# Warm-up, first transposes and one block fewer in halves: four small edits at the start of a fused convolution and two-layer kernel

## The chip, the cores and the metric

The kernel runs on one core of a Trainium2 chip. The metric is the device time of one execution in microseconds. A profile gives the span from the first to the last instruction, which is about 2 us less than the time of the same execution.

## The reference

A causal convolution of seven taps over the sequence, one set of softmax-normalised taps for each of eight heads, and then two matrix products with a leaky ReLU between them.

```python
w = softmax(weight, axis=-1)                       # 8 heads, 7 taps
out[b, s, h, :] = sum_k w[h, k] * x_pad[b, s + k, h, :]   # x: 8 x 4096 x 192
h = out.reshape(32768, 192) @ w_in                 # 192 x 2048
y = maximum(0.01 * h, h) @ w_out                   # 2048 x 192, fp32 out
```

## The kernel before

The sequence is cut into 32 blocks; a block is 512 positions of two batch rows. The first blocks are worked in halves of 256 positions, so that the first matmuls can start before much of x has arrived. After these the kernel passes to whole blocks and to another form of the second product.

```python
NHALF = 4
groups = [(b, h * HT, HT) for b in range(NHALF) for h in range(2)]
groups += [(b, 0, ST) for b in range(NHALF, NBLK)]
# ...
plan = {0: [0] * 4, NSW - 2: [16, 8, 8, 16], NSW - 1: [8, 8, 16, 16],
        NSW: [16, 8, 8, 16, 8, 8, 16, 16]}         # NSW = 2 * NHALF
```

At the very start TensorE runs warm-up matmuls while x and the taps are loaded. Then it selects the taps (a matmul with a 0/1 matrix spreads them over 128 partitions), transposes the first x into PSUM, and convolves the first half block by matmuls with diagonal matrices. VectorE and ScalarE build these diagonals and copy the transposed x out of PSUM.

```python
warm(6, ST)                          # six matmuls of 512 columns
select(wps_hm, slice(0, 2)); warm(1, 128)
select(wps_l, 2);            warm(1) # 256 columns
# ... casts of x, whm <- wps_hm
diag_wide(0, 0, K); diag_each(1, 1, range(2))
transpose_first(0)                   # six transposes 128x128, bf16 in PSUM
warm(1, ST)
evac_first(0, nc.scalar.copy, nc.vector.tensor_copy)
diag_wide(0, 1, K)                   # VectorE
for p in range(2): diag_wide(2, p, K)
spread_down(0)                       # VectorE, w_in within SBUF
# ... wml, rsum (VectorE): every evacuation of the convolution needs rsum
diag_each(1, 1, range(2, K)); diag_each(1, 0, range(K))   # ScalarE
# ... convolution: 84 matmuls; evac_0(act_scale), evac_2(...), evac_1(act_scale)
```

A "unit" is a group of twelve first-layer matmuls, followed by one ScalarE activation of 128x1024 (Prelu, PSUM to g). Two PSUM buffers `ph` are shared by the units. The third piece of x is transposed behind unit 7, the last of the first half block.

Of the kernel before, what the change touches and what calls it, by code (L numbers as in the profile page):

```python
# [10 lines left out]
FP32 = mybir.dt.float32  # L11
BF16 = mybir.dt.bfloat16
# [3 lines left out]
def kernel(  # L16
# [8 lines left out]
    nc = tc.nc  # L25
# [11 lines left out]
    NCH = D // CH  # L37
# [3 lines left out]
    HS = SUB // 2  # L41
    NFC = F // 128
    NB = S // ST
    NBLK = (B // 2) * NB
    NHALF = 4
    RUN = 4
    NPEC = 3
    FIRST = (0, 2, 1)
# [12 lines left out]
    psum_o = ctx.enter_context(tc.tile_pool(name="po", bufs=4, space=bass.MemoryType.PSUM))  # L61
# [5 lines left out]

    groups = [(b, h * HT, HT) for b in range(NHALF) for h in range(2)]
    groups += [(b, 0, ST) for b in range(NHALF, NBLK)]

# [34 lines left out]
    def new_xt(rp):  # L105
        xt[rp] = xt_pool.tile([128, NCH, HALO + S], BF16, name="xt")
        nc.vector.memset(xt[rp][:, :, 0:HALO], 0.0)
# [5 lines left out]
    x_half = {  # L113
        q: const_pool.tile([128, NCH, HS, 2, CH], BF16, name=f"x_half{q}") for q in (0, 3)
    }
# [27 lines left out]
    ptr = {}  # L143

    def transpose_first(q):
        n = HS if q == 0 else 1
        ts = [
            psum_o.tile([128, HS // n, NCH, 128], BF16, name=f"ptr{i}", tag="po")
            for i in range(n)
        ]  # L150
        for s in range(HS):
            t = ts[s * n // HS]
            for c in range(NCH):
                if q == 0:
                    nc.tensor.transpose(
                        out=t[:, 0, c, :],
                        in_=x_half[q][:, c, s, :, :].rearrange("p e k -> p (e k)"),
                        identity=ident,
                    )
                    continue  # L160
                for e in range(2):
                    nc.tensor.transpose(  # L162
                        out=t[e * CH : (e + 1) * CH, s, c, :],
                        in_=x_rows[q][:, e, s, c * CH : (c + 1) * CH],
                        identity=ident,
                    )
        ptr[q] = [t[:, s] for t in ts for s in range(HS // n)]

    def evac_first(q, *copies):
        dst = xt[0][:, :, HALO + q * HT : HALO + (q + 1) * HT]  # L170
        dst = dst.rearrange("p c (s k) -> p s c k", s=HS)
        for s, t in enumerate(ptr.pop(q)):
            copies[s](out=dst[:, s], in_=t)  # L173
# [13 lines left out]
    def conv_jobs(grp, chunks=range(NCH)):  # L187
        blk, t0, T = grp
        rp, st = divmod(blk, NB)
        if blk not in yt:  # L190
            yt[blk] = yt_pool.tile([128, NCH, ST], BF16, name="yt")
        y = yt[blk]
        jobs = []
        for k in range(K):
            for c in chunks:
                a = BASE + k + st * ST + t0
                src = xt[rp][:, c, a : a + T]
                dst = y[:, c, t0 : t0 + T]
                if k == 0:
                    jobs.append(  # L200
                        lambda s=src, d=dst, c=c: nc.vector.tensor_scalar_mul(  # L201
                            d, s, wk[:, c, 0:1]
                        )
                    )
                else:
                    jobs.append(
                        lambda s=src, d=dst, c=c, k=k: nc.vector.scalar_tensor_tensor(  # L207
                            out=d, in0=s, scalar=wk[:, c, k : k + 1], in1=d,
                            op0=mybir.AluOpType.mult, op1=mybir.AluOpType.add,
                        )  # L210
                    )
        return jobs
# [42 lines left out]
    def run(*lists):  # L255
        for slots in zip_longest(*lists, fillvalue=()):
            for both in slots:
                for job in both:
                    job()
# [31 lines left out]
    def spread_down(n):  # L291
        nc.vector.tensor_copy(out=w_in[n][0:CH, 1, :], in_=w_in[n][CH:128, 0, :])

    def spread_up(n):
        nc.vector.tensor_copy(out=w_in[n][CH:128, 1:3, :], in_=w_in[n][0:CH, 0:3:2, :])
# [10 lines left out]
    ident = const_pool.tile([128, 128], BF16)  # L306
# [3 lines left out]
    for rows in (0, 128):  # L310
# [7 lines left out]
        in_=moe_w_out.rearrange("(c p i) d -> p c i d", p=128, i=RUN),  # L318
# [7 lines left out]
    def warm(n, cols=HT):  # L326
        for _ in range(n):
            nc.tensor.matmul(  # L328
                out=wa[:, 0, 0:cols], lhsT=ones[:, 0:128], rhs=ones[:, 0:cols],
                start=True, stop=True,  # L330
            )
# [21 lines left out]
    ident2 = const_pool.tile([128, CH], BF16)  # L353
    nc.vector.tensor_add(ident2, ident[:, 0:CH], ident[:, CH:128])
    warm(6, ST)
    wps = psum_h.tile([128, 2, ST], FP32, name="wps", tag="ph")
    wps_hm = wps[:, 0, 0 : NCH * 2 * (K + 1)].rearrange("p (c q k) -> p c q k", c=NCH, q=2)
    wps_l = wa[:, 1, 0 : NCH * (K + 1)].rearrange("p (c k) -> p c k", c=NCH)

    def select(out, parts):  # L360
        for c in range(NCH):
            for e in range(2):
                nc.tensor.matmul(
                    out=out[e * CH : (e + 1) * CH, c], lhsT=sel[:, c, :],
                    rhs=w9p[:, parts, :], start=True, stop=True,
                )
# [1 line left out]
    select(wps_hm, slice(0, 2))  # L368
    warm(1, 128)
    select(wps_l, 2)  # L370
    warm(1)
    new_xt(0)
    cast_first(0, 0, nc.scalar.copy)
    cast_first(0, 1, nc.scalar.copy, slice(0, 1))
# [22 lines left out]
    diag_wide(0, 0, K)  # L397
    diag_each(1, 1, range(2))
    transpose_first(0)
    warm(1, ST)  # L400
    evac_first(0, nc.scalar.copy, nc.vector.tensor_copy)
# [38 lines left out]
    g, po, acc2, osb, seal = {}, {}, {}, {}, None  # L440
    NSW = 2 * NHALF
    subs = [
# [148 lines left out]
    def evac_o(n):  # L591
# [4 lines left out]
        o_sb = osb[n if n >= LAST else n - n % 2]  # L596
        copy = nc.scalar.copy if b < NHALF else nc.vector.tensor_copy
        ins = copy(out=o_sb[:, n % 2, :], in_=po.pop(n))  # L598
# [18 lines left out]
    for i, grp in enumerate(groups):  # L617
        blk, t0, T = grp
        steps = T // 64
        if t0 == 0:  # L620
            g[blk] = g_pool.tile([128, NFC, 2, ST], BF16, name="g", tag="g")
        quota = plan.get(i, [16] * 4 if T == HT else [5, 5, 6, 5, 5, 6, 8, 8])

        if i == 0:
            ahead = []
        else:
            ahead = conv_jobs(groups[i + 1]) if i + 1 < len(groups) else []
        per = -(-len(ahead) // steps)
        for j in range(steps):
            for u in range(2 * j, 2 * j + 2):  # L630
                mm1(grp, u, 128 if i <= NSW else CH)
                if i == 0 and u == 0:
                    conv_1 = conv_jobs(groups[1], (1,))
                    for job in conv_1[:3]:
                        job()
                    spread_down(1)
                    spread_up(1)
                    for job in conv_1[3:]:
                        job()
                    pe_0, evac_0 = pe_conv_jobs(groups[1], 0)  # L640
                    pe_2, evac_2 = pe_conv_jobs(groups[1], 2, cross=True)
                if i == 0 and u in CUTS:
                    cut = slice(*CUTS[u])
                    run(pe_0[cut], pe_2[cut])
                if i == 0 and u == 5:
                    evac_0(nc.vector.tensor_scalar_mul)
                    evac_2(nc.vector.tensor_scalar_mul, nc.vector.tensor_scalar_mul)
                if i == 0 and u == 7:
                    transpose_first(2)
            jobs = ahead[per * j : per * (j + 1)]  # L650
            if T == ST:


                jobs = ahead[len(ahead) * j // steps : len(ahead) * (j + 1) // steps]
                for job in jobs:
                    job()
                jobs = []
            for _ in range(quota[j]):
                if i <= NSW:
                    mm2_row_slot(slot)  # L660
                else:
                    mm2_slot(slot)
                slot += 1
            if i == 0 and j == 3:
                evac_first(2, nc.vector.tensor_copy, nc.vector.tensor_copy)
            if i == 2 and j == 1:
                transpose_x(2)
            for job in jobs:
                job()
            if i == 0 and j == 3:  # L670
                transpose_half(3)

            last_half = t0 + T == ST
            if i == NSW and j == steps - 1:
                evac_o(LAST - 1)
                slot = NSW * NR * NFC
            if j == steps // 4 and last_half:
                load_x(blk + 3)
            if j == steps // 2 and last_half and blk > 0:
                transpose_x(blk + 2)  # L680
# [35 lines left out]
```

## Time and profile before

| quantity | value | from |
|---|---|---|
| time | 685.11 us (684.30, 685.11, 686.15) | three timed runs |
| span of the profiled execution | 682.4 us (its time: 684.35) | profile |
| TensorE busy | 677.2 us | profile |
| first second-layer matmul starts | 19.77 us | timeline |
| a half block, steady | 10.52 us | window |
| a whole block, steady | 20.72 us | window |

TensorE is the bound, busy 677.2 of 682.4 us: everything after the first 20 us is matmul after matmul. Two questions are left for a change like this one: does it shorten the sum of matmuls, and does it bring the first second-layer matmul forward? The lines that show this are in the prediction below.

### The profile page before, as it was taken

The page shows a single profiled execution, that of the slowest core. Times are in us where ns is not written, and L with a number is a line of the kernel's source. Part 1 is how long each engine was busy: PE and PEld are TensorE (multiplying, and loading weights), DVE is VectorE, ACT ScalarE, POOL GpSimd, SP SyncE. Part 2 cuts the span into 40 slices and gives each one's busy share as a digit, 9 for nine tenths or more (in the row PEclk, how much of TensorE's full clock was granted, in tenths as well). Part 3 has the DMA queues.
Part 4 walks back from the last instruction along what each step waited for, and adds up shares of the span by engine and source line. Part 5 has one row for each costly group of instructions (what it writes and reads, how often), then busy time and mean ns, then how long its engine had stood idle before and what let it go on. Part 6 is the DMA issues. An engine that isn't in the chain of part 4 may idle for free.

```text
span 682.4 us, 27404 instructions
## 1 busy us (share of the span) xinstructions
PE 677.2 (99%) x12575; PEld 467.1 (68%) x12575; DVE 481.4 (71%) x845; ACT 524.2 (77%) x623; POOL 145.9 (21%) x204
## 2 busy tenths in 40 slices
PE   9999999999999999999999999999999999999998
PEld 6999987666666666666666666666666666666667
DVE  7979767667678667687667786676786676876612
ACT  7888998778777777777778777777777777777781
POOL 7722223222102222012222022221022220000000
PEclk9999999999999999999999999999999999999999
DMA  9965668556467557376565575574575573321123
GB/s 152 109 91 74 84 90 88 68 56 91 78 89 86 63 65 93 73 96 78 57 79 82 85 95 68 56 91 79 88 87 62 66 95 71 72 56 34 33 49 93
DMA packets 211763, 53.29 MB, mean 78 GB/s; under 512 B 205120, under 2 KB 211264, under 8 KB 211648
## 3 DMA queue, kind: packets, MB, share of 16 engines
q0 software_dynamic: 98736, 13.97, 31.0%
q1 hardware_dynamic: 112896, 37.57, 27.5%
q8 instruction: 98, 1.61, 1.0%
q14 instruction: 17, 0.14, 0.1%
q10 hardware_dynamic: 16, 0.00, 0.0%
HBM read 28.31 MB, written 25.17 MB: 78 GB/s over the span
## 4 chain that ended last, share of the span: by engine, by line
PE 97%; ACT 2%; DVE 0%; issue 0%; ACTq 0%
PE ph L461 48%; PE acc L550 41%; PE po L487 7%; ACT g L468 1%; PE acc L232 1%; PE ptr L162 0%; ACT L334 0%; ACTq L263 0%; ACT diag L391 0%; ACT xt L173 0%; DVE o_sb L598 0%; DVE x_half L138 0%; ACT w L340 0%; ACT junk L334 0%; DVE w9p L348 0%
## 5 line engine op out<-in xcount | busy, mean ns | idle before, releaser
L468 ACT ACTIVATE g<-ph 128x1024 bf16<-128x1024 f32 x512 | 496.2, 1021 | 136.4 <-PE ph L461 136.0
L207 DVE SCALAR_TENSOR_TENSOR yt<-xt,wk,yt 128x512 bf16<-128x512 bf16 (+1 forms) x618 | 382.9, 691 | 0.2
L461 PE MATMUL ph<-yt,w_in 64*64 64x512 bf16 (+2 forms) x6048 | 378.0, 363 | 0.7 <-ACT g L468 0.5
L550 PE MATMUL acc<-g,w_out 64*64 64x512 bf16 x5184 | 316.5, 376 | 0.0
L461 PEld LDWEIGHTS <-w_in 64*64 64x64 bf16 (+1 forms) x6048 | 239.1, 129 | 96.9 <-issue 2.8
L550 PEld LDWEIGHTS <-w_out 64*64 64x64 bf16 x5184 | 168.4, 119 | 108.4
L83 POOL DMA_DIRECT2D x_bf<-in_x_dram x180 | 134.1, 770 | 412.0 <-DMA xt<-x_bf 303.8
L572 DVE STREAM_TRANSPOSE o_t<-acc 128x512 f32<-128x512 f32 x81 | 67.2, 866 | 171.1 <-PE acc L550 171.1
L487 PE MATMUL po<-w_out,g 64*128 64x192 bf16 (+1 forms) x1152 | 60.1, 243 | 0.0
L487 PEld LDWEIGHTS <-g 64*128 64x128 bf16 (+1 forms) x1152 | 55.7, 94 | 1.6 <-issue 0.4
L201 DVE TENSOR_SCALAR yt<-xt,wk 128x512 bf16<-128x512 bf16 (+1 forms) x103 | 28.1, 322 | 14.5 <-DMA xt<-x_bf 14.4
L560 ACT COPY junk<-junk 128x1 f32<-128x1 f32 x54 | 10.4, 192 | 4.1 <-ACT g L468 0.4
L598 ACT COPY o_sb<-po 128x192 f32<-128x192 f32 x32 | 10.1, 320 | 1.3
L598 DVE COPY o_sb<-po 128x192 f32<-128x192 f32 x8 | 2.8, 356 | 6.8 <-PE po L487 4.0
L232 PE MATMUL acc<-xt,diag 64*64 64x256 bf16 x140 | 5.5, 272 | 0.4 <-ACT xt L173 0.4
L232 PEld LDWEIGHTS <-diag 64*64 64x64 bf16 x140 | 4.3, 106 | 1.5 <-DVE xt L173 0.7
L132 POOL DMA_DIRECT2D x_half<-in_x_dram x6 | 4.2, 720 | 1.2 <-DMA w_in<-in_moe_w_in_dram 1.2
L328 PE MATMUL warm<-const-bfloat16-1.0 128*128 128x512 bf16 (+2 forms) x9 | 3.6, 515 | 0.8 <-PEq L700 0.8
L391 ACT ACTIVATE diag<-ident,whm 128x64 bf16<-128x64 bf16 x14 | 3.5, 337 | 0.2 <-DVE whm L377 0.2
L128 POOL DMA_DIRECT2D x_rows<-in_x_dram x4 | 3.0, 751 | 0.0
L173 DVE COPY xt<-ptr 128x384 bf16<-128x384 bf16 x5 | 1.6, 352 | 1.8 <-PE ptr L162 1.7
L334 ACT ACT_TABLE_LOAD x1 | 1.3, 1283 | 1.4 <-PEq L700 1.4
(45 smaller groups left out, 22.5 us busy)
## 6 DMA issues: line engine op xcount, KB each, us to landing
out_dram<-o_t SPq DMA_DIRECT2D x108, 192.0 KB, 4.7
x_bf<-in_x_dram POOLq DMA_DIRECT2D x180, 64.0 KB, 3.3
out_dram<-o_sb SPq DMA_DIRECT2D x16, 192.0 KB, 3.2
xt<-x_bf SPq DMA_TRANSPOSE x90, 3.8
w_out<-in_moe_w_out_dram POOLq DMA_DIRECT2D x1, 768.0 KB, 9.4
out_dram<-o_sb SPq DMA_DIRECT2D x8, 96.0 KB, 1.9
w_in<-in_moe_w_in_dram POOLq DMA_DIRECT2D x2, 256.0 KB, 5.5
x_nat<-in_x_dram SPq DMA_DIRECT2D x2, 192.0 KB, 2.6
```

Of the source, the lines that this page charges most:

```text
L83: nc.gpsimd.dma_start(out=t[:, c, :, e, :], in_=src[2 * rp + e, :, :, c * CH : (c + 1) * CH],)
L132: nc.gpsimd.dma_start(out=x_half[q][:, c, :, e, :], in_=rows[:, e, :, c * CH : (c + 1) * CH],)
L201: lambda s=src, d=dst, c=c: nc.vector.tensor_scalar_mul(d, s, wk[:, c, 0:1])
L207: lambda s=src, d=dst, c=c, k=k: nc.vector.scalar_tensor_tensor(out=d, in0=s, scalar=wk[:, c, k : k + 1], in1=d, op0=mybir.AluOpType.mult, ...
L232: lambda k=k, p=p, a=a, ps=ps, to=to, acc=accs[e * apart]: nc.tensor.matmul(out=acc[to, :T], lhsT=diag[c][ps, p, k, :], rhs=xt[0][ps, c, a ...
L461: nc.tensor.matmul(out=ph[m : m + M, e, i * T : (i + 1) * T], lhsT=w_in_of(f, e, c, m, m + M), rhs=y[ps, c, t0 : t0 + T], start=(c == chun ...
L468: act = nc.scalar.activation(out=g[blk][:, nf * u : nf * (u + 1), :, t0 : t0 + T], in_=ph.rearrange("p e (i t) -> p i e t", i=nf), func=my ...
L487: return nc.tensor.matmul(out=po[m], lhsT=g[b][ps, fc, e, s * 128 : (s + 1) * 128], rhs=w_out[ps, fc, :], start=start, stop=stop,)
L550: ins = nc.tensor.matmul(out=acc2[gi, r][e * CH : (e + 1) * CH, 0:T], lhsT=w_out_of(ps, fc, r), rhs=g[b][ps, fc, e, t0 : t0 + T], start=fi ...
L560: seal = nc.scalar.copy(out=junk, in_=junk)
L572: nc.vector.transpose(out=osb[gi, 0][:, 0 : T // GB, :, r], in_=acc2.pop((gi, r))[:, 0:T].rearrange("p (j k) -> p j k", k=GB),)
L598: ins = copy(out=o_sb[:, n % 2, :], in_=po.pop(n))
```

## The change

Its intent is to save on the start. Identity matmuls take the place of the first six transposes, apparently for the sake of TensorE's clock. Short warm-ups fill gaps around the selection. The third transposes move into a pause of TensorE. And block 3 is worked whole.

```diff
-    NHALF = 4
+    NHALF = 3
@@ transpose_first
-            psum_o.tile([128, HS // n, NCH, 128], BF16, name=f"ptr{i}", tag="po")
+            psum_o.tile([128, HS // n, NCH, 128], BF16 if q else FP32, ...)
-                    nc.tensor.transpose(out=t[:, 0, c, :], in_=x_half[q]..., identity=ident)
+                    nc.tensor.matmul(out=t[:, 0, c, :], lhsT=x_half[q]..., rhs=ident,
+                                     start=True, stop=True)
@@
     warm(6, ST)
+    warm(2, 128)
@@
     select(wps_l, 2)
-    warm(1)
+    warm(2, 128)
@@
-                if i == 0 and u == 7:
+                if i == 0 and u == 6:
                     transpose_first(2)
```

(Two long lines are shortened.)

More of the change, by code (lines that the diff above doesn't have):

```diff
@@ L147, in transpose_first @@
         ts = [
-            psum_o.tile([128, HS // n, NCH, 128], BF16, name=f"ptr{i}", tag="po")
+            psum_o.tile(
+                [128, HS // n, NCH, 128], BF16 if q else FP32, name=f"ptr{i}", tag="po"
+            )
             for i in range(n)
@@ L154, in transpose_first @@
                 if q == 0:
-                    nc.tensor.transpose(
+                    nc.tensor.matmul(
                         out=t[:, 0, c, :],
-                        in_=x_half[q][:, c, s, :, :].rearrange("p e k -> p (e k)"),
-                        identity=ident,
+                        lhsT=x_half[q][:, c, s, :, :].rearrange("p e k -> p (e k)"),
+                        rhs=ident,
+                        start=True,
+                        stop=True,
                     )
```

## The prediction

> **What bounds the kernel now.** I read the page of the kernel before first, then the chain of waits, then the start of the timeline, then two windows in the steady part. The page says which engine fills the span:
>
> ```profile
> span 682.4 us, 27404 instructions
> PE 677.2 (99%) x12575; PEld 467.1 (68%) x12575; DVE 481.4 (71%) x845; ACT 524.2 (77%) x623; POOL 145.9 (21%) x204
> PE 97%; ACT 2%; DVE 0%; issue 0%; ACTq 0%
> ```
>
> TensorE is busy 677.2 of 682.4 us and carries 97% of the chain that ended last. Only 5.2 us of the span is without a matmul, so a change that only closes gaps cannot win 2% (13.7 us). Two stages matter: the first 20 us, where the chain leaves TensorE, and the steady stage, where time is simply the sum of matmuls. For the steady stage I compared two windows of one half block (256 positions of two batch rows) and two windows of one whole block (512 positions):
>
> ```profile
> 26.55:37.07 10.52, 10.52 (x228) 10.52 (x226) 8.39 (x24) 9.03 (x12) 3.45 (x5) 1.00 1.05 108
> 37.07:47.59 10.52, 10.52 (x228) 10.52 (x226) 8.61 (x25) 9.03 (x12) 4.45 (x6) 1.00 0.82 96
> 126.82:147.54 20.72, 20.72 (x390) 13.31 (x384) 15.03 (x26) 15.89 (x18) 4.46 (x6) 1.00 0.49 72
> 147.54:168.26 20.72, 20.72 (x390) 13.30 (x384) 15.01 (x25) 15.89 (x18) 4.28 (x6) 1.00 0.58 78
> ```
>
> After the window come its length and then the busy time of TensorE, its weight loads, VectorE, ScalarE and GpSimd. I cut the windows at points where the chain repeats (the first-layer group of 24 matmuls starts at 26.55, 37.07, 47.59; and, for whole blocks, at 126.82, 147.54, 168.26). TensorE fills all of them. A block in two halves costs 2 x 10.52 = 21.04 us, a whole block 20.72 us.
>
> The start of the kernel, TensorE, VectorE and ScalarE in order of time:
>
> ```profile
> 0.85 2.72 PE L328 MATMUL warm<-const-bfloat16-1.0 128*128 128x512 bf16 x6 [0.85 <-PEq L700]
> 4.77 0.38 PE L328 MATMUL warm<-const-bfloat16-1.0 128*128 128x512 bf16 x1
> 5.52 3.40 PE L232 MATMUL acc<-xt,diag 64*64 64x256 bf16 x84 [0.37 <-ACT xt L173]
> ...
> 5.06 0.35 DVE L173 COPY xt<-ptr 128x384 bf16<-128x384 bf16 x1
> ...
> 5.37 2.96 ACT L391 ACTIVATE diag<-ident,whm 128x64 bf16<-128x64 bf16 x12
> 8.24 1.45 ACT L419 ACTIVATE yt<-acc,rsum 128x256 bf16<-128x256 f32 x3
> ...
> 16.08 2.99 ACT L468 ACTIVATE g<-ph 128x1024 bf16<-128x1024 f32 x3 [0.32 <-PE ph L461]
> 17.16 0.85 PE L461 MATMUL ph<-yt,w_in 64*128 64x256 bf16 x12 [0.46 <-ACT g L468]
> 17.94 0.53 PE L162 MATMUL ptr<-ident,x_rows 128*64 128x128 bf16 x12
> 18.39 1.57 PE L461 MATMUL ph<-yt,w_in 64*128 64x256 bf16 x24
> ```
>
> What to see: the warm-up matmuls of 512 columns start 0.43 us apart at first (six lie in 2.72 us, with the modelled tail of the last), but one took only 0.38 us with its whole tail at 4.77. The array runs at half rate until about 3.5 us and at full rate after. The convolution by matmuls starts at 5.52, when the transposed x is out of PSUM, and ScalarE then works without a pause from 5.37 to 9.69. At 17.16 TensorE waits for ScalarE, which frees the two buffers of ph.
>
> [...] 0.43 us per 512 columns early, and by 3.84 to 4.19 us a 128-column warm-up matmul took 0.23 us and a 256-column one 0.28 us, that is 0.05 us for 128 more columns, or full rate. Whether other executions switch later, no profile here shows. [...] the twelve transposes at 17.94 end a group of 64*128 matmuls whose last stream ends near 17.85 and the next group starts at 18.39, 0.54 us for transposes whose own streams need 6 x 0.056 = 0.34 us. [...] VectorE copied 128x384 bf16 out of PSUM in 352 ns and 128x192 fp32 in 356 ns.
>
> **The change part by part.**
>
> *Three blocks in halves instead of four.* Block 3 becomes a whole block, and the passage from one scheme to the other moves one block earlier with the same plan of quotas (the plan is keyed to the end of the halves). So the sum loses 2 x 10.52 and gains 20.72: **-0.32 us**, all on TensorE, which is the path. VectorE gets easier: the convolution of a half block is 18 x 480 ns + 3 x 300 ns = 9.5 us, twice 19.1 us, against 18 x 738 + 3 x 327 ns = 14.3 us for a whole block. In the trace VectorE finished the eighth half at 69.8 and waited for transposed x until 73.10, so it runs ahead of TensorE; the first whole block's convolution ended at 87.7, 2.3 us before TensorE needed it at 89.96. After the change this pair lies at block 3, whose x is transposed while block 1 runs and was already used by its halves before; it has more room. For block 4, x is fetched at the same place of the program, TensorE needs it some 2 us sooner than before (the passage with its shorter quotas comes first), but VectorE has 4.8 us less to do. I expect no new wait.
>
> *First x by identity matmuls.* Six transposes become six matmuls of the same 128 columns: same TensorE time at the same clock. But a matmul writes fp32, so the two copies out of PSUM change. VectorE: fp32 copies from PSUM took 198 ns for 48 columns and 356 ns for 192, 1.10 ns a column, so 384 columns should take 356 + 192 x 1.10 = 0.57 us instead of 0.35: +0.22 us. ScalarE: 320 ns for 192 fp32 columns plus 192 x 0.83 ns (from its casts of 192 and 384 columns, 351 and 511 ns) = 0.48 us instead of 0.457: +0.02 us. So the first convolution matmul starts at about 5.67 instead of 5.52, and the second diagonal group (TensorE waited for VectorE's diag until 6.54) at 6.74. The convolution ends 0.2 us later. But what follows is ScalarE's chain: its last diag ends at 8.33, and it evacuates at 8.24, 8.72 and 9.22, the last needing a convolution that ended at 8.93 and will end at 9.13. That still fits. What reaches ScalarE is rsum, which VectorE makes at 7.9 and which ScalarE's first evacuation needs; VectorE there stood about 0.1 us for the w_in load, so of its 0.22 us about 0.1 reaches 8.24 and some of that is hidden by the last diag. **+0.07 us** on the path (estimate).
>
> *Warm-ups.* Two matmuls of 128 columns after the first six: 0.1 us each at half rate, from 3.36 on. The selection then loads its weights [...] near 3.67 instead of 3.49, and its matmuls wait for VectorE until 3.65 anyway; delay under 0.1 us. whm is copied at 4.29, behind VectorE's cast, 0.35 us after the selection had ended. The second pair replaces one matmul of 256 columns by two of 128, done by about 4.4; the first x starts at 4.42 because of its cast. **0 us** directly. The use is in the clock (below).
>
> *Third transposes ahead of the last unit.* They now stand after the matmuls of unit 6, which end streaming near 16.54, in the 0.46 us in which TensorE waited; 0.54 us from 16.54 ends at 17.08, before 17.16. So 0.54 us of TensorE is hidden, and the next group could start at 18.08 instead of 18.39. But its second unit needs ScalarE to finish unit 7, at 19.07, and it started at 19.13 before too (the 1.57 us of that group, against 1.51 usual, shows it). So the second-layer matmuls start at 19.8 in both: **0 us**. The gain ends at ScalarE.
>
> Sum for an execution with the clock as in this trace: -0.32 + 0.07 + 0 + 0 = **-0.25 us**.
>
> **The clock in other executions.** The three timed runs are 684.30, 685.11 and 686.15 us, the profiled one 684.35. [...] the convolution, 3.4 us of full-rate matmuls, runs partly at half rate, which could cost one to two us; that would explain 685 and 686. [...] The mean excess of the four runs over the lowest is (0.05 + 0 + 0.81 + 1.85)/4 = 0.68 us; I let about half of that go, -0.4 us. This is a choice, since no profile of a slow start exists. 685.11 - 0.25 - 0.4 = 684.5 us.
>
> **The rivals.** (1) The clock part is real and large: all runs start like the profiled one. Then the median is near 684.3 - 0.25 = 684.1. For it: the spread of 1.85 us in runs with nothing else to vary but DMA. Against: nothing shows the clock of those runs. (2) VectorE's fp32 copy becomes the bound: if ScalarE's copy also slows, the whole start slides by 0.2 us or more and the change nets zero, near 685.0. For it: VectorE has no pause from 3.25 to 7.0. Against: ScalarE's slack of 0.25 us before the last evacuation. (3) The third transposes do pay, because the unit wait at 19.13 is not ScalarE's: then 0.3 us more, 684.2. Against: ScalarE is continuous from 16.08 to 19.07. (4) A new wait at block 3 or 4 for transposed x: 1 to 3 us, 686 to 687. Against: xt waits had no TensorE wait behind them before, and VectorE gains time.
>
> **Range and chances.** The parts on the path are below 0.4 us each, and run-to-run spread is 1.9 us. A median of a few runs should lie between 683.5 and 685.6. Faster by 2% would need 13.7 us, more than all TensorE idle time: 0.003. Slower by 2% would need a stall in every block: 0.004. The rest is within 2%.
>
> **What would show it.** Right: span near 682.1 in the profile if the clock rises as early; one whole block less in halves, with windows still 10.52 and 20.72 full; VectorE's first xt copy near 0.57 us, the convolution starting near 5.67, the first g of ScalarE still within 0.1 us of 10.41; transposes near 16.6 and the second-layer matmuls still near 19.8. Wrong: the second-layer matmuls starting much before 19.7 (the transposes or the start did pay) or after 20.1, a TensorE wait on yt between 68 and 110 us, or a spread of the timed runs as wide as before (the clock was not what spread them).

## The result

The changed kernel took 684.36 us (median of six, 684.24 to 686.01), the kernel before 685.40 us in the same comparison (median of six, 684.30 to 686.15). The ratio is 0.9991 with a 95% interval of 0.9978 to 1.0004: the same, at the 2% that is asked. A ratio is the mean time of one kernel's runs over that of the other's in the same rounds, so it is not quite the ratio of the medians quoted. Here the means differ by less than the medians, because both kernels have runs near 684.3 and runs near 686.

The profiled execution of the changed kernel happened to be its slowest, 686.01 us. Its page, in the lines that answer to those of before:

```profile
span 684.3 us, 27253 instructions
PE 679.5 (99%) x12514; PEld 458.0 (67%) x12514; DVE 482.4 (70%) x827; ACT 522.2 (76%) x617; POOL 146.0 (21%) x204
PE 98%; ACT 2%; DVE 0%; issue 0%
```

The matmuls are fewer by 61, yet TensorE was busy 2.3 us longer. The chain is the same: TensorE. The timeline of the start shows where the time is:

```profile
4.62 0.84 PE L157 MATMUL ptr<-ident,x_half 128*128 128x128 bf16 x6
5.26 0.63 PE L332 MATMUL warm<-const-bfloat16-1.0 128*128 128x512 bf16 x1
6.12 5.16 PE L236 MATMUL acc<-xt,diag 64*64 64x256 bf16 x84 [0.22 <-DVE xt L177]
21.25 0.85 PE L466 MATMUL ph<-yt,w_in 64*128 64x256 bf16 x12 [0.20 <-ACT g L473]
21.91 1.52 PE L492 MATMUL po<-w_out,g 64*128 64x192 bf16 x32
```

The columns are start, duration, engine, line, operation, out<-in, tile and shape, count, and the idle time before with what ended it. The six identity matmuls took 0.84 us, where the six transposes of before took 0.51. The warm-up took 0.63 us against 0.38, and the convolution 5.16 us against 3.40. The start ran at half rate for longer (the identity matmuls started 0.106 us apart, where in the run by turns below matmuls of the same size at the full clock started 0.056 us apart): the trace's clock record, which tells from when on TensorE was granted its full clock, begins at 10.07 us for this execution and at 3.53 us in the profile of before. So these two profiles must not be compared as they stand. A second profile of the changed kernel, taken later with five more timed runs, has its clock record from 4.17 us (time 684.20), and can be set beside before:

```profile
5.11 0.55 DVE L177 CAST xt<-ptr 128x384 bf16<-128x384 f32 x1
...
5.71 3.45 PE L236 MATMUL acc<-xt,diag 64*64 64x256 bf16 x84 [0.50 <-DVE xt L177]
7.29 0.53 DVE L296 COPY w_in<-w_in 64x1024 bf16<-64x1024 bf16 x1
...
8.54 1.47 ACT L424 ACTIVATE yt<-acc,rsum 128x256 bf16<-128x256 f32 x3 [0.16 <-PE acc L236]
```

```profile
16.94 0.53 PE L166 MATMUL ptr<-ident,x_rows 128*64 128x128 bf16 x12
17.47 1.76 PE L466 MATMUL ph<-yt,w_in 64*128 64x256 bf16 x24
19.43 0.85 PE L466 MATMUL ph<-yt,w_in 64*128 64x256 bf16 x12 [0.20 <-ACT g L473]
20.09 1.15 PE L492 MATMUL po<-w_out,g 64*128 64x192 bf16 x23
```

```profile
26.85:37.37 10.52, 10.52 (x229) 10.52 (x226) 7.32 (x19) 9.02 (x13) 2.76 (x4) 1.00 0.90 100
126.92:147.64 20.72, 20.72 (x392) 13.20 (x388) 15.05 (x26) 15.89 (x18) 4.46 (x6) 1.00 0.78 82
```

VectorE's first copy takes 0.55 us (0.35 before), ScalarE's first evacuation starts at 8.54 (8.24 before), and the first second-layer matmul at 20.09 (19.77 before). Two lines of before to set beside them:

```profile
7.04 0.42 DVE L292 COPY w_in<-w_in 64x1024 bf16<-64x1024 bf16 x1
...
19.77 1.52 PE L487 MATMUL po<-w_out,g 64*128 64x192 bf16 x32
```

From there the steady windows are as full as before. The single rows of the two traces give the sum, from start to start: from the first to the last second-layer matmul before took 678.985 - 19.769 = 659.216 us and the changed kernel 678.981 - 20.085 = 658.896 us. So at an equally early clock the start lost 0.32 us and the rest won 0.32 us, and the last second-layer matmul starts at the same time in both.

The times of these two executions still differ, 684.35 against 684.20, through two stretches that this sum leaves out. From the end of the last second-layer matmul to the end of the span it is 3.19 us before and 3.27 us in the changed kernel. And the time exceeds the span by 1.93 us before and by 1.71 us in the changed kernel. The second difference is no accident of two executions: it is 1.92 us on average with four blocks in halves (36 runs, 1.79 to 2.01) and 1.73 us with three (38 runs, 1.66 to 1.98). With the prelude described below, three blocks in halves alone take it from 1.98 to 1.73 us (four runs each). So about 0.2 us of what the change gains lies outside the span, where no profile looks, and comes with the three blocks in halves; why is open.

### The profile page after: what moved, and what is told of

It is laid out like the page before. It is cut to its first block, busy times and chain, and to the rows that moved or that the text cites. A ratio compares the mean times of both kernels' runs of the same rounds, so it can differ in the third digit from the quotient of the medians.

```text
span 684.3 us, 27253 instructions
## 1 busy us (share of the span) xinstructions
PE 679.5 (99%) x12514; PEld 458.0 (67%) x12514; DVE 482.4 (70%) x827; ACT 522.2 (76%) x617; POOL 146.0 (21%) x204
## 4 chain that ended last, share of the span: by engine, by line
PE 98%; ACT 2%; DVE 0%; issue 0%
PE ph L466 48%; PE acc L555 42%; PE po L492 6%; ACT g L473 2%; PE acc L236 1%; PE warm L332 1%; PE ptr L157 0%; DVE xt L177 0%; PE ptr L166 0%; DVE o_sb L603 0%; PE wps L368 0%; PE warm L368 0%
## 5 line engine op out<-in xcount | busy, mean ns | idle before, releaser
L555 PE MATMUL acc<-g,w_out 64*64 64x512 bf16 x5376 | 328.2, 376 | 0.0
L466 PEld LDWEIGHTS <-w_in 64*64 64x64 bf16 (+1 forms) x6048 | 234.4, 130 | 101.3 <-issue 2.3
L555 PEld LDWEIGHTS <-w_out 64*64 64x64 bf16 x5376 | 172.4, 118 | 114.6
L577 DVE STREAM_TRANSPOSE o_t<-acc 128x512 f32<-128x512 f32 x84 | 70.6, 885 | 175.3 <-PE acc L555 175.3
L492 PE MATMUL po<-w_out,g 64*128 64x192 bf16 (+1 forms) x896 | 48.0, 243 | 0.0
L492 PEld LDWEIGHTS <-g 64*128 64x128 bf16 (+1 forms) x896 | 44.5, 95 | 1.6 <-issue 0.4
L603 ACT COPY o_sb<-po 128x192 f32<-128x192 f32 x24 | 7.6, 320 | 0.8
L236 PE MATMUL acc<-xt,diag 64*64 64x256 bf16 x140 | 7.3, 338 | 0.2 <-DVE xt L177 0.2
L332 PE MATMUL warm<-const-bfloat16-1.0 128*128 128x512 bf16 (+1 forms) x12 | 4.2, 492 | 0.8 <-PEq L705 0.8
```

The source lines that it names most:

```text
L236: lambda k=k, p=p, a=a, ps=ps, to=to, acc=accs[e * apart]: nc.tensor.matmul(out=acc[to, :T], lhsT=diag[c][ps, p, k, :], rhs=xt[0][ps, c, a ...
L332: nc.tensor.matmul(out=wa[:, 0, 0:cols], lhsT=ones[:, 0:128], rhs=ones[:, 0:cols], start=True, stop=True,)
L466: nc.tensor.matmul(out=ph[m : m + M, e, i * T : (i + 1) * T], lhsT=w_in_of(f, e, c, m, m + M), rhs=y[ps, c, t0 : t0 + T], start=(c == chun ...
L492: return nc.tensor.matmul(out=po[m], lhsT=g[b][ps, fc, e, s * 128 : (s + 1) * 128], rhs=w_out[ps, fc, :], start=start, stop=stop,)
L555: ins = nc.tensor.matmul(out=acc2[gi, r][e * CH : (e + 1) * CH, 0:T], lhsT=w_out_of(ps, fc, r), rhs=g[b][ps, fc, e, t0 : t0 + T], start=fi ...
L577: nc.vector.transpose(out=osb[gi, 0][:, 0 : T // GB, :, r], in_=acc2.pop((gi, r))[:, 0:T].rearrange("p (j k) -> p j k", k=GB),)
```

## The experiments

Twelve runs follow, two of them of the two kernels unchanged. The first four carry a prelude, the next eight do not. In what follows "clock" is the start of the full-rate record in the trace, in us from the start of the span.

### A prelude, to take the clock out

Thirty-two warm-ups of 512 columns run first, and the first load of every queue waits for them; the six old warm-ups become twelve. The four kernels differ only in what follows. Abridged:

```diff
+    for _ in range(32): matmul(wa[:, 0, :], ones[:, 0:128], ones)
+    gate <- wa (VectorE); first element of w9, x_nat and sel <- gate
     nc.scalar.dma_start(out=w9[:, 0:K], in_=weight)
@@
-    warm(6, ST)
+    warm(12, ST)
```

**The kernel before with the prelude.**

> The kernel before with a prelude: 32 warm-up matmuls of 512 columns run first, and the first loads of every queue wait for them, so the array should be at full clock when the old start begins (and 12 warm-ups in place of 6 keep it busy). Theory 1 (the clock's switch spreads the times): the spread of the timed runs shrinks from 1.9 us to under 0.6 us, the convolution's 84 matmuls take 3.4 us from first start to last end, as in the fast profile, and the time is near 684.3 plus a prelude of some 9 us. Rival (the spread comes from transfers or elsewhere): the spread stays near 1.5 to 2 us.

Measured: 694.03 us median, 693.37 to 694.99. The 84 matmuls took the expected 3.40 us, but the spread did not shrink to 0.6 us: it was 1.62 us, as the rival said. The expectation failed by my own design: the prelude's slow part is itself inside the time. Dense warm-ups began at 0.85 us in all four kernels with this prelude, and the clock records begin at 3.73, 6.68, 6.49 and 6.24 us; the selection, which comes after the same work, starts at 12.66, 14.10, 13.99 and 13.88. Each is later than the first by about half of its clock's delay (1.44 us for 2.95, for example), as half rate makes it. So the clock's switch moves by about 3 us from one execution to the next under the same load, and that alone is worth 1.4 us. The timed medians of these four kernels can't be used for tenths of a microsecond, but their profiles can, from a point after the prelude on.

**The changed kernel with the prelude.**

> The changed kernel with the same prelude. Theory 1: with the clock out of play, it is 0.25 us faster than the kernel before with the prelude (0.32 from the halves, less 0.07 for the fp32 copies). Rival A (the fp32 copies cost their whole 0.2 us or more): the difference is 0.1 us or less. Rival B (the third transposes pay too): 0.5 us or more.

Measured: 693.73 us median, 693.53 to 694.94, against 694.03: 0.3 us, inside the spread, so the medians decide nothing. In the profile VectorE waited 1.15 us for the second half of w_in to land, and so the start up to the first second-layer matmul grew by another half microsecond. The same wait is at most 0.42 us in the other profiles with the prelude, so this belongs to that execution's loads. From the first to the last second-layer matmul it took 658.90 us.

**Three blocks in halves alone, with the prelude.**

```diff
-    NHALF = 4
+    NHALF = 3
```

> The kernel before with the prelude and three blocks in halves, and nothing else of the change. Theory 1: 0.32 us faster than the kernel before with the prelude. Rival (the passage to whole blocks costs more when it comes a block earlier): less than 0.15 us faster, with a wait of TensorE between 68 and 100 us after the prelude.

Measured: 694.33 us median, 693.86 to 694.51; by the clock record (6.49) its profile started 1.34 us late. From the first to the last second-layer matmul: 658.89 us, against 659.22 with four blocks in halves. That is -0.32 us, what 2 x 10.52 - 20.72 gives, and there is no wait of TensorE at the passage that the kernel before hasn't got. All thirteen profiles but the run by turns (both of before, both of the changed kernel, and nine edits) fall into two groups here: 659.21 to 659.22 us with four blocks in halves, 658.89 to 658.90 with three. The rival falls.

**The changed kernel with real transposes, with the prelude.**

```diff
-                    nc.tensor.matmul(out=t[:, 0, c, :], lhsT=x_half[q]..., rhs=ident, ...)
+                    nc.tensor.transpose(out=t[:, 0, c, :], in_=x_half[q]..., identity=ident)
```

> The changed kernel with the prelude, but with the first x by real transposes again (bf16 in PSUM). Theory 1: 0.05 to 0.1 us faster than the changed kernel with the prelude, since VectorE's copy goes from 0.56 back to 0.35 us and most of that was hidden. Rival A: 0.2 us or more faster. Rival C (nothing reaches the path): equal within 0.03 us.

Measured: 693.96 us median, 693.57 to 694.87, against 693.73: nothing to be had from the medians. The timelines of VectorE and ScalarE do tell. First the changed kernel with the prelude, then this one:

```profile
14.64 0.20 DVE L392 COPY whm<-wps 128x48 f32<-128x48 f32 x1
...
15.41 0.55 DVE L176 CAST xt<-ptr 128x384 bf16<-128x384 f32 x1
15.88 1.68 DVE L398 TENSOR_TENSOR diag<-ident,whm 128x448 bf16<-128x448 bf16 x3
17.59 0.42 DVE L308 COPY w_in<-w_in 64x1024 bf16<-64x1024 bf16 x1
...
18.73 1.47 ACT L434 ACTIVATE yt<-acc,rsum 128x256 bf16<-128x256 f32 x3
```

```profile
14.46 0.20 DVE L390 COPY whm<-wps 128x48 f32<-128x48 f32 x1
...
15.23 0.35 DVE L174 COPY xt<-ptr 128x384 bf16<-128x384 bf16 x1
15.50 1.69 DVE L396 TENSOR_TENSOR diag<-ident,whm 128x448 bf16<-128x448 bf16 x3
17.22 0.42 DVE L306 COPY w_in<-w_in 64x1024 bf16<-64x1024 bf16 x1
...
18.41 1.46 ACT L432 ACTIVATE yt<-acc,rsum 128x256 bf16<-128x256 f32 x3
```

From the copy of whm to ScalarE's first evacuation it is 4.10 us with fp32 and 3.95 us with bf16 (single rows: 4.096 and 3.952; 3.950 in both other prelude kernels with bf16). The copy itself costs 0.20 us more, 0.15 us of it arrives at the evacuation. In both, w_in is copied 0.03 us after the last diagonal ends: VectorE does not wait for w_in there.

### Without the prelude

**The kernel before, once more.**

> The kernel before, unchanged, to get a second profile and more times. Theory 1 (the clock's switch sorts the times): if the profiled execution takes over 685 us, its clock record starts after 5.5 us and the convolution's 84 matmuls take over 4 us; if it takes about 684.3 us, the record starts near 3.5 us and they take 3.4 us. Rival (loads of weights and x landing late): a slow execution shows the same 3.4 us and a wait for a transfer instead.

Measured: 685.85 us median of five, 684.28 to 686.01. The profiled execution took 685.32, and its clock record begins at 7.95:

```profile
5.21 0.63 PE L328 MATMUL warm<-const-bfloat16-1.0 128*128 128x512 bf16 x1
5.87 4.25 PE L232 MATMUL acc<-xt,diag 64*64 64x256 bf16 x84
```

The 84 matmuls took 4.25 us, as theory 1 expected of a slow execution. A late clock therefore slows the kernel before too.

**The changed kernel, once more.**

> The changed kernel, unchanged, for a second profile and more times. From the first second-layer matmul to the end it takes what the first profile shows, 0.32 us less than before. Theory 1: more than half of its times lie at 684.0 to 684.5 us, and a slow one has a late clock record. Rival: the times spread evenly over 684.2 to 686.2 us like those of before.

Measured: 684.63 us median of five, 684.20 to 685.86, ratio 0.9998 (0.9986 to 1.0010). Two of the five lie in the expected 684.0 to 684.5, with the first six runs six of eleven. With the first six, seven of eleven times lie at 684.20 to 684.63 and four at 685.17 to 686.01; the pooled median is 684.38. The profile is the one with the early clock that is shown above.

**Changed kernel, real transposes, no prelude.** The edit is the one of the prelude's last kernel.

> The changed kernel with the first x by real transposes again; the extra warm-ups, the three blocks and the earlier third transposes stay. Theory 1 with transposes that do not count for the clock: its fast runs are 0.1 us below those of the changed kernel (about 684.1), but fewer of its runs are fast. Rival (transposes count like matmuls, or the count hardly matters): as many fast runs, and a median at or below that of the changed kernel.

Measured: 684.22 us median of five (684.02, 684.21, 684.22, 684.52, 685.24), ratio 0.9990 (0.9978 to 1.0002). Its three fastest average 684.15 us, the changed kernel's six below 684.5 average 684.30; with its fourth, 684.52, it is 684.24. As many runs are fast, so identity matmuls are not needed for that. The profiled execution was the slowest one, and not by the clock (5.69) alone:

```profile
9.71 0.24 PE L164 MATMUL ptr<-ident,x_rows 128*64 128x128 bf16 x1 [0.33 <-DMA x_rows<-in_x_dram]
10.30 0.52 PE L164 MATMUL ptr<-ident,x_rows 128*64 128x128 bf16 x11 [0.35 <-DMA x_rows<-in_x_dram]
```

Here TensorE waited for the second piece of x to land. So a late load is a second source of slow executions, seen once; the rival of transfers is right in part.

**Changed kernel with one more warm-up behind the first x.**

```diff
     transpose_first(0)
-    warm(1, ST)
+    warm(2, ST)
```

> The changed kernel with two warm-up matmuls of 512 columns instead of one behind the first x, which fill the 0.4 us in which TensorE waits for the copies out of PSUM. In the slow profile the clock did not rise at about 6.7 us[...]. Theory 1: with the gap filled it rises there or earlier, so no run is over 685.3 us and the median is near 684.3. Rival: times spread as before, 1 us or more above 684.3.

Measured: 684.37 us median of six: five at 684.24 to 684.51, one at 686.35. The expectation that no run would be over 685.3 failed. The profiled execution (684.33, clock 4.37) was a fast one, so what made 686.35 was not seen. The extra warm-up cost nothing.

**The warm-ups alone.**

```diff
     warm(6, ST)
+    warm(2, 128)
@@
-    warm(1)
+    warm(2, 128)
```

> The kernel before with the two pairs of 128-column warm-ups and nothing else of the change. So far 8 of 30 times of before lie under 684.45 us, and 16 of 22 of three kernels that all have these warm-ups under 684.5. Theory 1 (the warm-ups bring the clock up in time in more executions): at least half of the runs lie at 684.2 to 684.5 us, as the fast ones of before. Rival (the identity matmuls or the third transposes did it): they spread like those of before, median near 685.4.

Measured: 684.86 us median of four (684.60, 684.81, 684.90, 686.34), ratio 1.0002 (0.9988 to 1.0017). None lies at 684.2 to 684.5, so the expectation failed in its size; three of four lie below 685, as ten of thirty of before do. The profile (684.81) has no clock record, but its warm-up at 5.25 us took 0.61 us and its convolution 3.45 us, so the clock rose between these.

**The identity matmuls alone.** The edit is that of the change to the first transposes, and nothing else.

> The kernel before with the first x by identity matmuls into fp32, and nothing else of the change. Theory 1 (fp32 copies delay rsum and with it ScalarE's first evacuation): its fast runs lie near 684.6 us, 0.3 above the fast ones of before, and VectorE's copy takes 0.55 us. Rival (identity matmuls count for the clock where transposes do not, and that is what moved the median): most runs are fast and the median is near 684.6, against 685.4.

Measured: 685.88 us median of four (684.67, 685.73, 686.03, 686.46), ratio 1.0007 (0.9993 to 1.0022). Only one is fast, and it lies 0.37 us above the fast ones of before (684.30 on average). The profiled one (686.03) has its clock at 9.14. The rival, that the identity matmuls bring the clock up, gets no support.

**The parts that paid, together.** The changed kernel with real transposes and with the second 512-column warm-up.

```diff
-                    nc.tensor.matmul(...)   # first x
+                    nc.tensor.transpose(...)
@@
-    warm(1, ST)
+    warm(2, ST)
```

> The changed kernel with real transposes for the first x and with two 512-column warm-ups behind them: the parts that paid, without the one that cost. Theory 1: fast runs at 684.0 us, 0.3 below those of the changed kernel, most runs fast, median 684.1. Rival (only identity matmuls hold the clock up): fast runs as low but fewer, median over 684.5.

Measured: 684.31 us median of four (684.09, 684.31, 684.31, 686.19), ratio 0.9994 (0.9981 to 1.0007). The three fast ones average 684.24, not the expected 684.0, and it is not measurably better than the changed kernel. The profiled one (684.31) has its clock at 5.64, and its first second-layer matmul, at 20.18, is 0.4 us behind that of before at an early clock.

**Transposes and matmuls by turns.**

```diff
+    160 transposes, 128 identity matmuls, 160 transposes of ident (128x128 bf16)
     ident2 = const_pool.tile([128, CH], BF16)
     warm(6, ST)
```

> The kernel before with 160 transposes, then 128 identity matmuls, then 160 transposes of the same 128x128 bf16 matrix ahead of the selection. If transposes do not count as busy for the clock: the first 160 start about 107 ns apart to their end, the matmuls go from 107 to 56 ns after some 3.5 us or so, and the clock may fall again in the last 160. If they count: the first 160 go to 56 ns within 3.5 to 7 us and all that follows stays there.

Measured: 711.6 us, one run. The timeline:

```profile
3.17 10.64 PE L358 MATMUL pa<-ident 128*128 128x128 bf16 x160 [3.17 <-POOL ident masks.py:199]
13.64 7.31 PE L360 MATMUL pb<-ident 128*128 128x128 bf16 x128
20.79 9.10 PE L358 MATMUL pa<-ident 128*128 128x128 bf16 x160
```

The second 160 transposes took 9.10 us, 56 ns each from start to start, and so did the 128 matmuls before them (7.31 us): this is the full rate. The first 160 took 10.64 us; at half rate throughout they would have taken 160 x 0.107 = 17.1 us (an estimate: 0.107 us is a quarter of the 0.43 us between the first 512-column warm-ups of before). The clock record begins 3.25 us after the first transpose, with nothing but transposes before it, and the clock does not fall during the last 160. So in this run transposes alone brought the clock up. In the four kernels with the prelude, where 512-column matmuls alone stand at that place, the record begins 2.9 to 5.8 us after the first of them.

### All profiled starts in one table

| kernel | time us | clock from | 84 convolution matmuls | first second-layer matmul | from it to the last one |
|---|---|---|---|---|---|
| before | 684.35 | 3.53 | 3.40 | 19.77 | 659.22 |
| changed, second profile | 684.20 | 4.17 | 3.45 | 20.09 | 658.90 |
| changed + warm-up | 684.33 | 4.37 | 3.46 | 20.09 | 658.90 |
| parts that paid | 684.31 | 5.64 | 3.39 | 20.18 | 658.90 |
| changed, real transposes | 685.24 | 5.69 | 3.46 | 21.00 (load late) | 658.90 |
| warm-ups alone | 684.81 | 5.3 to 5.9 | 3.45 | 20.18 | 659.21 |
| before, second profile | 685.32 | 7.95 | 4.25 | 20.75 | 659.22 |
| identity alone | 686.03 | 9.14 | 4.73 | 21.43 | 659.22 |
| changed, first profile | 686.01 | 10.07 | 5.16 | 21.91 | 658.90 |

The last column has two values, fixed to 0.01 us. Apart from the two stretches outside this table (together, with the last matmul itself, 5.2 to 5.4 us), all else that separates two executions happens in the first 22 us, and there it goes with the clock, with one late load as the exception.

## Why the prediction was right, and where it was not

The time fell where it was predicted: 684.36 us, predicted 684.5 in a range of 683.5 to 685.6. "Within 2%" held. That the number came so near is in part luck: of its two parts, the -0.25 us for an equal clock was made up otherwise than predicted, and the -0.4 us was a choice.

Some of the prediction's own signs went against it. At an early clock the span was 682.5 us, not 682.1, and ScalarE's first g came at 10.73, not within 0.1 us of 10.41. The six timed runs of the changed kernel spread over 1.77 us, as widely as those of before (1.85 us), which was to mean that the clock was not what spread them; yet the profiles show that it was. The steps fared as follows.

**Halves, -0.32 us: right.** It is shown by the edit alone and by every profile. The 0.2 us outside the span, which comes with it, was not foreseen.

**Third transposes, 0: right, by the way that was told.** They lie at 16.94 in the pause of TensorE. The ninth activation of ScalarE starts 8.55 us after the first instead of 8.87, but the first second-layer matmul comes 9.36 us after that first activation, in all nine profiles without a prelude (with it, 9.36 to 9.89). The gain ends at ScalarE, as the prediction said: TensorE waits for it at 19.43. The place was not undone by itself in a run; four of these nine profiles have the old place and five the new one.

**Identity matmuls, "+0.07 us on the path (estimate)": wrong in size.** At an early clock the first evacuation of ScalarE came 0.30 us later, and the first second-layer matmul 0.32 us. The duration of the copies was right (0.57 us expected, 0.55 measured; ScalarE's took 0.46 to 0.48 us with either type). The step that failed is "VectorE there stood about 0.1 us for the w_in load". It did not: the copy of w_in follows the last diagonal by 0.03 us in every profile, so VectorE absorbed nothing. The delay goes from the copy to the diagonals, to w_in, to rsum, and from rsum to ScalarE; the convolution's own slack, which the prediction looked at, does not matter. Of the 0.20 us, 0.05 us is hidden behind ScalarE's last diagonals, as the prediction said: with bf16 ScalarE goes from them to the evacuation without a pause, 0.15 us after rsum is done, and with fp32 it waits and starts 0.10 us after rsum. So of the 0.30 us, 0.15 are this chain (the prelude pair), 0.05 a later start of VectorE's copy (5.11 against 5.06), and 0.11 a slower copy of w_in (0.53 instead of 0.42). The last was seen in both profiles without a prelude that have an early clock and fp32 copies, and in no other; why is open. The timed runs do not settle the cost: fast runs with real transposes are 0.15 us faster if three of them are counted, and 0.06 us if four.

So up to the last second-layer matmul the sum for an equal clock was not -0.25 but about 0: -0.32 from the halves, and +0.3 at the start where the fp32 copies stand. The -0.15 us between the times of the two executions lies in the stretches after it and outside the span, which the prediction did not look at.

**The clock, -0.4 us, called a choice: its size is not shown, and nothing shows a part of the identity matmuls in it.** The spread does come from the clock's switch, which no profile had shown at the time. Over all comparisons the mean of before is 685.27 us (30 timed runs) and of the changed kernel 684.84 us (11). That is 0.43 us, with a standard error of 0.25 us, and about 0.2 us of it lies outside the span. The fast runs of the two average 684.30 us each, so as a count the gain is that more executions are fast: 7 of 11 below 685 us against 10 of 30. Chance alone makes a difference like that in about one of seven such comparisons (exact test). Five kernels have the short warm-ups, and 22 of their 30 timed runs lie below 685; of before and the identity matmuls alone it is 11 of 34, and here chance is unlikely (0.001). Four of the five also have three halves; if their times are put back by what the halves gain and the fp32 copies cost, 21 of 30 remain. (The line at 685 was drawn after the times were seen; there is a gap from 684.90 to 685.11.) Real transposes do as well as identity matmuls in this (four of five runs of the changed kernel with real transposes lie below 685), and in the run by turns the clock came up 3.25 us after the first transpose, so nothing here makes the identity matmuls part of the cause. The halves and the third transposes come after 16 us, when the full clock had been granted in every profile (10.07 us at the latest). The likely cause is therefore the short warm-ups in the gaps. That is argued, not shown: it is supported by the pooled count, and not by the run of the warm-ups alone, whose four runs (three below 685) are too few. What decides when the clock rises was not shown: in the first profile of the changed kernel it rose only at 10.07 us, and with one warm-up more one of six runs still took 686.35 us.

The rivals: (1), all runs of the changed kernel start fast, fell with its first profile; (2), the fp32 copies cancel the gain, is what the early-clock profiles show up to the last second-layer matmul, though by rsum and not by ScalarE's copy; (3) and (4) fell, there is neither a gain from the third transposes nor a wait at block 3 or 4.

## What to carry to other kernels

Before a tenth of a microsecond is booked at a kernel's start, find out in which clock state each profile was taken: two executions of one kernel can differ there by more than the whole change (here 684.20 and 686.01 us for the changed kernel, against 1.04 us between the medians). When a copy gets slower, follow everything that its engine does next down to the next engine's first wait, and look at the gap before each instruction to see whether slack was there at all. And a part that exists for a reason about the hardware is worth one direct test of that reason: here the run by turns showed that real transposes brought the clock up as well, 3.25 us after the first of them, so the fp32 detour was not needed for that. Compare time minus span between the kernels as well: part of a gain can lie where the profile does not look, as 0.2 us did here.
